# Seven-block products in single-bank PSUM tiles with four groups in flight

## The chip, the cores and the metric

The kernel runs on one core of a Trainium2 chip. The time is what the device takes for one execution, in microseconds (us); the median of several runs is given. The core's engines work side by side, each through its own list of instructions in order, and wait for each other by semaphores: TensorE (PE in the profile, with the weight loads as PEld), VectorE (DVE), ScalarE (ACT), GpSimd (POOL) and SyncE (SP). PE writes its results to PSUM, a memory of eight banks; here one bank holds 512 float32 numbers in each of 128 partitions. DVE and ACT read PSUM and write to the on-chip memory SBUF.

## The reference

```python
batch, n_heads, seq, head_dim = (8, 12, 448, 64)      # d_model = 768, d_ff = 3072

scores = scale * np.matmul(q, k.transpose(0, 1, 3, 2))
attn = np.maximum(scores, 0.0) ** 2 / S
attn_out = np.matmul(attn, v)

x = attn_out.transpose(0, 2, 1, 3).reshape(B, S, H * D)
xn = (x - mu) / np.sqrt(var + 1e-06) * g_ln
ch = np.maximum(xn @ w_ch1, 0.0) @ w_ch2
out = x + ch
```

`mu` and `var` are the mean and the variance over the 768 features of a row. Inputs and output are float32; the kernel multiplies in bfloat16 and sums in float32.

## The kernel before

Eight batches are worked through one after the other. For each there are the attention, the centring of its output, the first feed-forward product (the rows times w_ch1, then relu, into the activations `h1`) and the second (`h1` times w_ch2, scaled by the row's 1/sqrt(var) and added to x). The division by the standard deviation is pulled out of the first product and done at the end. Attention of a later batch is laid between the feed-forward steps of an earlier one. The last batch has no such filler left: its first product stands alone, and the last pass of second products follows it.

**Who sets the order.** The whole program is recorded by a planner, `Order`. Work for PE is added one step at a time by `pe`; work for the other engines is put in a list by `add`, with a cost, its dependencies and a key, and the planner commits it when its planned clocks say that it is next. The result is one fixed list for each engine. The planner's costs and due times decide only this order; on the chip, an instruction waits for the semaphores of what it reads and writes, and for all that stands ahead of it on its engine.

**The stage of the change.** For the last batch the first product is done by a scheme with seven block products in place of eight. The 24 column blocks of w_ch1 make six groups (`G4 = 6`). A group covers 4 x 128 columns of the output and all 448 rows of x; its output is cut in 2 x 2 blocks C11, C12, C21, C22 (two column halves, two halves of 224 rows). The products are P1, P2, P6, P5, P7, P3 and P4, each of 2 x 3 matmuls of 128x128 weights with 224 columns. Their operands are blocks or sums of blocks, made ahead on DVE: S1 to S4 of the weights (`make_w1_sums`), T1 to T4 of the rows (`make_x_sums`). In a group they run in four stages (`STAGES`): P1 P2, then P6 P5, then P7 P3, then P4. Two PSUM accumulators are used, x (P1, then P6, P7 and P4 added on) and y (P2; then P5 anew; then P3 added on). Between the stages:

- `keep` copies on ACT (L1128): c1 is x after P1, c2 is x after P6, p5 is y after P5; c1 and p5 go to a tile `v_t`, c2 to `at_all`, three places each.
- `add_relu` adds on DVE (L1112), with the relu in the same instruction: C11 = relu(y + c1) after P2, C22 = relu(x + p5) after P7, C12 = relu(y + c2) after P3.
- `relu` on ACT (L1141): C21 = relu(x) after P4.

P6 needs c1 (its accumulator may only be written on once the copy is taken), P5 needs C11, P7 needs c2, P3 needs p5, and P4 needs C22. Both accumulators of a group lie in one tile of two banks, from a pool `ps_s` of three such tiles that attention uses too. Two more banks, the pool `ps_f` (`f_tile`, `f_banks`), serve the other feed-forward products. The order of the stages over the groups is made beforehand by `fs_steps`, which plays the groups through with three places (`free`), 575 ns for a product and a given time until a group may go on.

**The last pass.** After the six groups, `ffn_w` does the second product for two pairs of row tiles with seven block products each (`PRODUCTS`), 12 matmuls of 384 columns to a product, in two halves (L1331; at the very end L1397). Its operands S1 to S4 are differences of activations, made on DVE (L1287); its results are taken out of PSUM by DVE (L1339), with the reciprocal root `r_t` (L805 on ACT, L807 on DVE, from the statistics L795 to L797) and stored by DMAs that ACT and SP issue (L1460). The statistics read rows of x that SP transposes by DMA (L772). For the pass before, the lines are L1422 and L1438.

`hold(slot_use)` marks a PSUM tile as taken until the group's last readers are known. `ops["h", b, i]` says to the planner when block i of the activations is ready.

Of the kernel before, what the change touches and what calls it, by code (L numbers as in the profile page):

```python
# [202 lines left out]
def kernel(  # L203
# [11 lines left out]
    P = 128  # L215
    bf16 = mybir.dt.bfloat16
    fp32 = mybir.dt.float32
# [3 lines left out]
    B, H, S, D = q.shape  # L221
# [26 lines left out]
    v_pool = ctx.enter_context(tc.tile_pool(name="v", bufs=1))  # L248
    xc_pool = ctx.enter_context(tc.tile_pool(name="xc", bufs=1))
    s_pool = ctx.enter_context(tc.tile_pool(name="small", bufs=4))  # L250
    ps_s = ctx.enter_context(tc.tile_pool(name="ps_s", bufs=3, space=bass.MemoryType.PSUM))
    ps_f = ctx.enter_context(tc.tile_pool(name="ps_f", bufs=1, space=bass.MemoryType.PSUM))

    identity = const_pool.tile([P, P], bf16)
    eps_sb = const_pool.tile([P, 1], fp32)
# [6 lines left out]
    sum_t = const_pool.tile([P, S], fp32)  # L262
# [29 lines left out]
    stage, vt, qkT, xc, xm, mvs, rstd = {}, {}, {}, {}, {}, {}, {}  # L292
    ops = {}
# [152 lines left out]
    slots = [DONE] * 3  # L446

    f_banks = [DONE] * 2
    f_tags = ["f0", "f1"]

    def f_tile(shape, dtype, **kw):

        f_tags.append(f_tags.pop(0))
        f_ps = ps_f.tile(shape, dtype, tag=f_tags[-1], **kw)
        return f_ps
# [11 lines left out]
    def hold(use):  # L467

        h = [PENDING]
        use(h)  # L470
        return h
# [3 lines left out]
    def later(*key):  # L475

        return later_ops.setdefault(key, [PENDING])

    def now_known(op, *key):
        later(*key)[:] = [op]  # L480
# [405 lines left out]
    def h_cols(b):  # L886
        return slice(T, T + S) if b % 2 == 0 else slice(0, S)
# [74 lines left out]
    G4 = K2 // 4  # L962
    SH = S // 2
    KQ = K1 // 2
    w1q = {}
    w1_todo = []
    f1q = {}

    def w1_block(g, row, k_half):
        return w1[:, k_half * KQ:(k_half + 1) * KQ, (4 * g + 2 * row) * P:(4 * g + 2 * row + 2) * P]  # L970
# [75 lines left out]
    W_OF = {"P1": ("A", 0, 0), "P2": ("A", 0, 1), "P6": "S2", "P5": "S1", "P7": "S3", "P3": "S4", "P4": ("A", 1, 1)}  # L1046
    X_OF = {"P1": "B11", "P2": "B21", "P6": "T2", "P5": "T1", "P7": "T3", "P3": "B22", "P4": "T4"}

    def fs_steps(b):

        order, live, t, nxt, free = [], {}, 0.0, 0, [0.0] * 3
        while nxt < G4 or live:
            ready = sorted(g for g, (st, r) in live.items() if r <= t)
            if ready:
                g = ready[0]
            elif nxt < G4 and min(free) <= t:
                g = nxt
                free.remove(min(free))
                live[g] = (0, t)
                nxt += 1  # L1060
            else:
                t = min([r for _, r in live.values()] + ([min(free)] if nxt < G4 and free else []))
                continue
            st = live.pop(g)[0]
            order.append(("fs", b, g, st))
            t += 575.0 * len(STAGES[st])
            if st < 3:
                live[g] = (st + 1, t + 1100.0)
            else:
                free.append(t + 1000.0)  # L1070
        return order

    def fs_deps(b, g, st, p=0):
        e = f1q.get(g, {})
        name = STAGES[st][p]
        w = W_OF[name]
        d = [ops["w1q", g, w] if isinstance(w, str) else None, ops["xq", X_OF[name]] if X_OF[name] in ("T1", "T2", "T3", "T4") else None]
        if st == 0:
            return [x for x in d if x is not None] + [ops["xc", b]] + ([slots[0]] if p == 0 else [])
        before = {"P6": "c1", "P5": "C11", "P7": "c2", "P3": "p5", "P4": "C22"}[name]  # L1080
        return [x for x in d if x is not None] + [e[before]]

    def ffn_1_seven(b, g, st):

        e = f1q.setdefault(g, {})
        for p, name in enumerate(STAGES[st]):
            bank = "x" if name in ("P1", "P6", "P7", "P4") else "y"

            def emit(eng, name=name, bank=bank):
                if name == "P1":  # L1090
                    ps = ps_s.tile([P, 2, 512], fp32, tag="s")
                    for i, x in enumerate("xy"):
                        e["ps", x] = ps[:, i, :S].rearrange("p (a c) -> p a c", a=2)
                w, x = W_OF[name], xq[X_OF[name]]
                a = w1q[g, w] if isinstance(w, str) else w1_block(g, *w[1:])
                for n in range(2):
                    for k in range(KQ):
                        nc.tensor.matmul(e["ps", bank][:, n, :], a[:, k, n * P:(n + 1) * P], x[:, k, :],  # L1098
                                         start=name in ("P1", "P2", "P5") and n == 0 and k == 0, stop=k == KQ - 1,
                                         skip_group_check=True)  # L1100
            op = R.pe(575.0, emit, fs_deps(b, g, st, p))
            e[name] = op
            if name == "P1":
                e["slot"] = hold(slot_use)
        c0 = h_cols(b).start

        def h_out(row, half):
            return h1[:, 4 * g + 2 * row:4 * g + 2 * row + 2, c0 + half * SH:c0 + (half + 1) * SH]

        def add_relu(key, row, half, bank, i1, deps):  # L1110
            def emit(eng):
                nc.vector._custom_dve(TENSOR_ADD_SAT, out=h_out(row, half), in0=e["ps", bank], in1=kept(i1), s0=float("inf"), s1=0.0)  # L1112
            e[key] = R.add("DVE", 620.0, emit, deps + [e[i1]], key=-3.0)

        def kept(name):
            if name == "c2":
                o = 3 * 2 * P + 3 * KQ * SH + (g % 3) * 2 * S
                t = at_all[:, o:o + 2 * S].bitcast(fp32)
            else:
                if "v" not in f1q:  # L1120
                    v_t = v_pool.tile([P, 3, S], fp32, tag="v1")
                    f1q["v"] = v_t
                t = f1q["v"][:, g % 3]
            return t.rearrange("p (a c) -> p a c", a=2)

        def keep(name, bank, deps):
            def emit(eng):
                nc.scalar.copy(kept(name), e["ps", bank])  # L1128
            e[name] = R.add("ACT", 560.0, emit, deps + [later("av_done", b)], key=-3.0)
        if st == 0:  # L1130
            keep("c1", "x", [e["P1"]])
            add_relu("C11", 0, 0, "y", "c1", [e["P2"]])
        elif st == 1:
            keep("c2", "x", [e["P6"]])
            keep("p5", "y", [e["P5"]])
        elif st == 2:
            add_relu("C22", 1, 1, "x", "p5", [e["P7"]])
            add_relu("C12", 0, 1, "y", "c2", [e["P3"]])
        else:
            def relu(eng):  # L1140
                nc.scalar.activation(h_out(1, 0), e["ps", "x"], Act.Relu)  # L1141
            e["C21"] = R.add("ACT", 560.0, relu, [e["P4"]], key=-3.0)
            e["slot"][:] = [e["C12"], e["C21"]]
            for i in range(4):
                ev = [e["C11"], e["C12"]] if i < 2 else [e["C21"], e["C22"]]
                ops["h", b, 4 * g + i] = ev
                later("h", b, 4 * g + i)[:] = ev
            if g == G4 - 1:
                ops["f1_end", b] = op
# [359 lines left out]
    def av_of(n):  # L1509
        return [("AV", n, s) for s in range(J)]  # L1510
# [118 lines left out]
    with tc.manual_schedule():  # L1629
# [32 lines left out]
        for c in FIRST_ORDER:  # L1662
            p = (av_stream if c == "a" else qk_stream).pop(0)
# [24 lines left out]
        for b in range(2, B):  # L1688
            u = b // 2
            vis = []  # L1690
            if b + 1 < B:
                n0 = (b + 1) * NPER
                for n in range(n0, n0 + NPER):
                    w = period(n, n > n0 or b > 2, False)
                    vis += w[1:] if n == n0 and b > 2 else w
                vis += [period(n0 + NPER, True, False)[0]] if b + 2 < B else [av_of(n0 + NPER - 1)]
            hooks = [(0, lambda b=b: load_batch(b + 2))] if b + 2 < B else []
            if b == 2:
                now_known(later("f2_out", 0), "s2_free", 1, 0)
            f2 = fw_steps(u, [0]) + f2_steps(u, [2]) if b % 2 == 0 else fw_steps(u, [3, 5])  # L1700
            for m in [0] if b % 2 == 0 else [3, 5]:
                pair_start(u, m)
            f1 = f1_steps(b)
            if b == LAST_B - 1:
                hooks = [(2, make_w1_sums)] + [(i, next_w1_sum) for i in range(4, 4 + 2 * 10, 2)] + [
                    (K2 + i, next_w1_sum) for i in range(14)]
            elif b == LAST_B:
                while w1_todo:
                    next_w1_sum()
                make_x_sums(b)  # L1710
                f1 = fs_steps(b)
            segment(f1 + f2, vis, b + 1 if b + 1 < B else None, 9000.0, hooks=hooks)
        R.drain()

# [29 lines left out]
```

## Time and profile before

| | us |
|---|---|
| three runs | 523.95, 523.54, 523.76 |
| median | 523.76 |
| the profiled execution, its own time | 524.23 |
| span in it, from the first to the last instruction | 522.5 |
| the last batch's seven-block products, first matmul to the last pass | 464.55 to 491.29 |
| the last pass on PE, with its closing products | 491.29 to 518.8 |

The other groups of this stage, by line, engine, operation and shape (tile names, shapes and count; busy us and mean ns of one; idle time of the engine before them and who ended it):

```profile
L1112 DVE CUSTOM_DVE_ANT_0 h<-ps,v_t 128x448 bf16<-128x448 f32 x12 | 7.4, 620 | 8.4 <-PE ps L1098 6.0 <-ACT v_t L1128 2.3
L1128 ACT COPY v_t<-ps 128x448 f32<-128x448 f32 x12 | 6.4, 535 | 8.1 <-PE ps L1098 8.1
L1128 ACT COPY at_all<-ps 128x448 f32<-128x448 f32 x6 | 3.2, 532 | 3.4 <-PE ps L1098 3.4
L1141 ACT ACTIVATE h<-ps 128x448 bf16<-128x448 f32 x5 | 2.7, 543 | 7.0 <-PE ps L1098 6.9
```

A row such as the first says: twelve adds on DVE, 620 ns each, 7.4 us in all; ahead of them DVE stood idle for 8.4 us, of which 6.0 were ended by PE's products and 2.3 by ACT's copies. The length of a matmul in the profile is modelled and reaches over the start of the next one, so how far apart two matmuls are is read from their starts.

### The profile page before, as it was taken

What the parts mean: (1) busy time and instruction counts of PE and PEld (TensorE: products, weight loads), DVE (VectorE), ACT (ScalarE), POOL (GpSimd) and SP (SyncE); (2) the same over time, 40 slices, a digit from 0 to 9 for tenths busy, and PEclk for the clock granted to TensorE, in tenths of its full rate; (3) what the DMA queues carried; (4) which work ended last, traced back from release to release, by engine and by line L of the source; (5) the groups of instructions that cost most, each with busy time, mean ns of one, the idle gap of its engine ahead of it and who ended that gap; (6) DMA issues with size and microseconds to landing.
All of it is one profiled execution on the core that took longest, in us unless ns stands there. A gap on an engine that the chain in (4) does not pass through costs nothing.

```text
span 522.5 us, 10193 instructions
## 1 busy us (share of the span) xinstructions
PE 507.8 (97%) x4200; PEld 285.9 (55%) x4200; DVE 371.1 (71%) x693; ACT 226.8 (43%) x365; POOL 116.4 (22%) x130
## 2 busy tenths in 40 slices
PE   5899999999999999999999999999999999999997
PEld 3444455555555455554555555554556555578764
DVE  5988647738897768774878667848488677968653
ACT  5977622116314663265522564336541476123300
POOL 6420700301141312321250311503211012300000
PEclk9999999999999999999999999999999999999999
DMA  9999999997279901989059960989224400231022
GB/s 193 197 186 195 202 195 155 172 126 105 63 113 184 100 7 19 166 128 107 15 102 113 128 78 15 148 122 95 38 39 93 92 0 1 54 83 19 1 60 62
DMA packets 144602, 51.85 MB, mean 99 GB/s; under 512 B 121894, under 2 KB 142764, under 8 KB 144556
## 3 DMA queue, kind: packets, MB, share of 16 engines
q0 software_dynamic: 81072, 25.50, 45.6%
q1 hardware_dynamic: 58844, 18.82, 21.7%
q10 hardware_dynamic: 4640, 6.88, 4.5%
q8 instruction: 33, 0.54, 0.4%
q14 instruction: 13, 0.11, 0.1%
HBM read 51.91 MB, written 11.01 MB: 120 GB/s over the span
## 4 chain that ended last, share of the span: by engine, by line
PE 89%; DVE 7%; ACT 2%; DMA 1%; issue 1%; SPq 0%; DVEq 0%; ACTq 0%
PE f_ps L934 37%; PE f_ps L1331 25%; PE f_ps L1422 10%; PE sc L590 6%; PE ps L653 5%; PE ps L1098 3%; DVE at_all L614 2%; DMA f<-in_k_dram 1%; DVE h L1112 1%; ACT at_all L599 1%; DVE a L863 1%; PE ps L510 1%; DVE h L1287 1%; DVE t L369 0%; DVE x_all L1209 0%
## 5 line engine op out<-in xcount | busy, mean ns | idle before, releaser
L934 PE MATMUL f_ps<-a,w 128*128 128x448 bf16 x990 | 193.1, 353 | 0.0
L934 PEld LDWEIGHTS <-w 128*128 128x128 bf16 x990 | 94.2, 98 | 94.0 <-issue 9.0
L599 ACT ACTIVATE at_all<-sc 128x896 bf16<-128x896 f32 x115 | 100.6, 924 | 70.5 <-PE sc L590 70.3
L950 ACT ACTIVATE h<-f_ps 128x448 bf16<-128x448 f32 (+1 forms) x138 | 72.4, 525 | 87.0 <-PE f_ps L934 85.3
L614 DVE TENSOR_TENSOR at_all<-at_all 128x896 bf16<-128x896 bf16 x157 | 98.7, 665 | 3.1 <-ACT at_all L599 3.0
L1331 PEld LDWEIGHTS <-h 128*128 128x128 bf16 x708 | 68.5, 98 | 47.9 <-issue 3.2
L601 DVE TENSOR_SCALAR at_all<-sc 128x896 bf16<-128x896 f32 x44 | 47.9, 1088 | 41.0 <-PE ps L653 23.6
L1331 PE MATMUL f_ps<-w,h 128*128 128x384 bf16 x360 | 62.5, 326 | 0.0
L590 PE MATMUL sc<-t 64*64 64x448 bf16 x672 | 49.4, 367 | 2.9 <-DVE t L369 1.5
L744 POOL TENSOR_TENSOR sum_t<-sum_t,xT_all 128x384 f32<-128x384 f32 (+2 forms) x25 | 20.9, 834 | 87.8 <-ACT xT_all L367 87.8
L1422 PE MATMUL f_ps<-w,h 128*128 128x384 bf16 x240 | 40.3, 326 | 0.0
L1339 DVE SCALAR_TENSOR_TENSOR o_all<-f_ps,r_t,x_all 128x384 f32<-128x384 f32 x39 | 24.0, 615 | 14.8 <-PE f_ps L1331 14.5
L590 PEld LDWEIGHTS <-t 64*64 64x64 bf16 x672 | 18.7, 107 | 27.8 <-issue 19.6
L1422 PEld LDWEIGHTS <-h 128*128 128x128 bf16 x240 | 23.2, 98 | 16.1 <-issue 1.1
L367 ACT CAST xT_all<-ps 128x768 bf16<-128x768 f32 (+2 forms) x32 | 19.9, 630 | 25.8 <-PE ps L653 23.7
L653 PE MATMUL ps<-at_all,v_t 64*64 64x448 bf16 x552 | 29.8, 350 | 0.0
L407 POOL DMA_DIRECT2D t<-in_k_dram x12 | 20.0, 1899 | 42.3 <-DMA t<-t 42.0
L742 POOL TENSOR_TENSOR sum_t<-xT_all 128x384 f32<-128x384 bf16 (+2 forms) x13 | 10.9, 860 | 81.8 <-ACT xT_all L367 81.5
L1339 DVE SCALAR_TENSOR_TENSOR o_all<-f_ps,r_t,o_all 128x384 f32<-128x384 f32 x30 | 18.4, 614 | 13.5 <-PE f_ps L1331 13.3
L653 PEld LDWEIGHTS <-v_t 64*64 64x64 bf16 x672 | 19.7, 107 | 13.5 <-issue 2.8
L407 POOL DMA_DIRECT2D t<-in_q_dram x12 | 19.3, 1772 | 32.9 <-DMA t<-t 29.8
L389 POOL DMA_DIRECT2D v_t<-in_v_dram x16 | 10.7, 674 | 63.1 <-PE sc L590 46.0
(135 smaller groups left out, 530.7 us busy)
## 6 DMA issues: line engine op xcount, KB each, us to landing
v_t<-in_v_dram POOLq DMA_DIRECT2D x16, 336.0 KB, 6.4
w<-in_moe_w_ch_dram POOLq DMA_DIRECT2D x4, 1152.0 KB, 37.9
out_dram<-o_all ACTq DMA_DIRECT2D x43, 96.0 KB, 2.8
t<-in_q_dram POOLq DMA_DIRECT2D x12, 336.0 KB, 7.8
t<-in_k_dram POOLq DMA_DIRECT2D x12, 336.0 KB, 6.8
out_dram<-o_all SPq DMA_DIRECT2D x35, 96.0 KB, 2.3
w<-in_moe_w_ch_dram POOLq DMA_DIRECT2D x4, 768.0 KB, 19.6
out_dram<-o_all ACTq DMA_DIRECT2D x13, 192.0 KB, 2.7
```

The lines of the kernel that those rows point to most:

```text
L407: nc.gpsimd.dma_start(stage["cols"][half * T:(half + 1) * T, t if b < 4 else 0].rearrange("p j (h d) -> p j h d", d=D), src[b, half * 6:ha ...
L590: nc.tensor.matmul(sc[rows_of(half), r, :S], qkT[b][rows_of(r), 1, s * NPER + pn, rows_of(half)], qT[:, :, pn, rows_of(half)], start=True, ...
L599: nc.scalar.activation(attn[n, s], st[0][:, :, :S], Act.Relu, scale=rc2)
L601: nc.vector.tensor_scalar(attn[n, s], st[0][:, :, :S], rc2, 0.0, op0=Alu.mult, op1=Alu.max)
L614: nc.vector.tensor_mul(attn[n, s], attn[n, s], attn[n, s])
L653: nc.tensor.matmul(av_st[n][half][rows_of(hh)], vt[b][rows_of(half), 2 * pn + hh, s * D:(s + 1) * D], attn[n, s][rows_of(half), hh, :], st ...
L744: nc.gpsimd.tensor_add(s0, s0, x0)
L934: nc.tensor.matmul(st[0], w1[:, ki, ni * P:(ni + 1) * P], xc[b][:, ki, :], start=(i == 0), stop=(i == K1 - 1))
L950: nc.scalar.activation(o, st[0][:, c], Act.Relu)
L1331: nc.tensor.matmul(e["ps", bank], a(k), w(k), start=new and k == 0, stop=k == KH - 1, skip_group_check=True)
L1339: nc.vector.scalar_tensor_tensor(o, e["ps", bank], r, o if more else xm[u, m + tile_n][:, cols], op0=Alu.mult, op1=Alu.add)
L1422: nc.tensor.matmul(o_st["ps"], stat(u, m, ki), w2[:, ki, j * hd:(j + 1) * hd], start=(ki == 0), stop=(ki == K2 - 1))
```

## The change

Five things are done. (1) A group's accumulators x and y become two tiles of one bank each, from a new pool `ps_n` that is opened in the place of `ps_s` when that is closed, at the first group; a tile of it waits only for what used its own memory. (2) Four groups may be under way in place of three (`FLIGHT`); the fourth of them, group 3, takes the two `ps_f` banks and a fourth place for the kept copies (`sum_t`, and a fourth part of `at_all`). (3) `fs_steps` counts on 1700 ns in place of 1100 and 1000 until a group may go on or its place is free (`AWAY`). (4) A block of activations counts as ready only with all blocks ahead of it. (5) The first half product of the last pass is laid ahead of the last block of the seven-block stage. The pool `ps_f` is now opened before `ps_s`, so the two change banks.

```diff
-    ps_s = ctx.enter_context(tc.tile_pool(name="ps_s", bufs=3, space=bass.MemoryType.PSUM))
     ps_f = ctx.enter_context(tc.tile_pool(name="ps_f", bufs=1, space=bass.MemoryType.PSUM))
+    s_banks = ctx.enter_context(ExitStack())
+    ps_s = s_banks.enter_context(tc.tile_pool(name="ps_s", bufs=3, space=bass.MemoryType.PSUM))
...
+    FLIGHT = 4
+    AWAY = 1700.0
+
     def fs_steps(b):
-        order, live, t, nxt, free = [], {}, 0.0, 0, [0.0] * 3
+        order, live, t, nxt, free = [], {}, 0.0, 0, [0.0] * FLIGHT
...
-            elif nxt < G4 and min(free) <= t:
+            elif nxt < G4 and free and min(free) <= t:
...
             if st < 3:
-                live[g] = (st + 1, t + 1100.0)
+                live[g] = (st + 1, t + AWAY)
             else:
-                free.append(t + 1000.0)
+                free.append(t + AWAY)
         return order
+
+    def in_f_banks(g):
+        return g == FLIGHT - 1
...
         if st == 0:
-            return [x for x in d if x is not None] + [ops["xc", b]] + ([slots[0]] if p == 0 else [])
+            return [x for x in d if x is not None] + [ops["xc", b]] + ([] if p else list(f_banks) if in_f_banks(g) else [slots[0]])
...
                 if name == "P1":
-                    ps = ps_s.tile([P, 2, 512], fp32, tag="s")
-                    for i, x in enumerate("xy"):
-                        e["ps", x] = ps[:, i, :S].rearrange("p (a c) -> p a c", a=2)
+                    if in_f_banks(g):
+                        x_ps = f_tile([P, S], fp32)
+                        y_ps = f_tile([P, S], fp32)
+                    else:
+                        if "pool" not in f1q:
+                            s_banks.close()
+                            f1q["pool"] = s_banks.enter_context(tc.tile_pool(
+                                name="ps_n", bufs=1, space=bass.MemoryType.PSUM, reuse_waits="tile"))
+                        x_ps = f1q["pool"].tile([P, S], fp32, tag=f"x{g % FLIGHT}")
+                        y_ps = f1q["pool"].tile([P, S], fp32, tag=f"y{g % FLIGHT}")
+                    for x, o in (("x", x_ps), ("y", y_ps)):
+                        e["ps", x] = o.rearrange("p (a c) -> p a c", a=2)
...
             if name == "P1":
-                e["slot"] = hold(slot_use)
+                e["x free"], e["y free"] = [hold(f_use) for _ in range(2)] if in_f_banks(g) else [hold(slot_use)] * 2
...
             if name == "c2":
-                o = 3 * 2 * P + 3 * KQ * SH + (g % 3) * 2 * S
+                o = 3 * 2 * P + 3 * KQ * SH + (g % FLIGHT) * 2 * S
                 t = at_all[:, o:o + 2 * S].bitcast(fp32)
             else:
...
-                t = f1q["v"][:, g % 3]
+                t = sum_t if g % FLIGHT == 3 else f1q["v"][:, g % FLIGHT]
...
-            e["slot"][:] = [e["C12"], e["C21"]]
+            e["x free"][:] = [e["C12"], e["C21"]]
+            e["y free"][:] = [e["C12"], e["C21"]]
+            f1q["out"] = ev = f1q.get("out", []) + [e[c] for c in ("C11", "C12", "C21", "C22")]
             for i in range(4):
-                ev = [e["C11"], e["C12"]] if i < 2 else [e["C21"], e["C22"]]
                 ops["h", b, 4 * g + i] = ev
...
                 f1 = fs_steps(b)
+                f1[-1:-1] = [f2.pop(0)]
             segment(f1 + f2, vis, b + 1 if b + 1 < B else None, 9000.0, hooks=hooks)
```

## The prediction

> **What bounds the kernel now.** I read the page first, then the busy table of the changed stage, then the order of its instructions in time, then the chain of waits.
>
> ```profile
> PE 507.8 (97%) x4200; PEld 285.9 (55%) x4200; DVE 371.1 (71%) x693; ACT 226.8 (43%) x365; POOL 116.4 (22%) x130
> PEclk9999999999999999999999999999999999999999
> PE 89%; DVE 7%; ACT 2%; DMA 1%; issue 1%; SPq 0%; DVEq 0%; ACTq 0%
> ```
>
> TensorE (PE) is busy for 97% of the span at full granted clock, so only time in which PE stands still can be won. The change touches one stage, the seven-block products of the last batch (L1098). It begins at 464.55 us and the last pass (L1331) follows it at 491.29. Busy time of PE, PEld (the weight loads), DVE, ACT and POOL in that stretch, then clock and DMA:
>
> ```profile
> 464.55:491.29 26.74, 25.42 (x254) 24.13 (x253) 17.63 (x36) 11.85 (x24) 0.00 (x0) 1.00 0.20 38
> ```
>
> There are 42 blocks (six groups of seven products) of six matmuls each. How long a block takes, and where PE stands, is read from starts, in the list of instructions by time:
>
> ```profile
> 467.71 0.74 PE L1098 MATMUL ps<-a,t 128*128 128x224 bf16 x6
> 468.29 0.74 PE L1098 MATMUL ps<-at_all,big_t 128*128 128x224 bf16 x6
> 468.86 0.74 PE L1098 MATMUL ps<-a,big_t 128*128 128x224 bf16 x6
> ...
> 471.23 0.74 PE L1098 MATMUL ps<-a,big_t 128*128 128x224 bf16 x6
> ...
> 472.16 0.73 PE L1098 MATMUL ps<-at_all,w 128*128 128x224 bf16 x6 [0.20 <-DVE h L1112]
> ```
>
> A block that follows without a stop starts 0.575 us after the one before (0.58, 0.57). 471.23 to 472.16 is 0.93, a stop of 0.36, of which the row admits 0.20: the drawn length of a matmul holds its way through the array. Over the whole stage: 42 x 0.575 = 24.15, and 26.74 - 24.15 = **2.59 us of stops**. Start by start they are 0.29 (at 467.14), 0.07, 0.36, 0.64 (at 476.25), 0.07, 0.36, 0.35, 0.07, 0.30 and 0.11, in sum 2.62. From 491.29 on, 156 matmuls of 384 columns take 25.35 us to 516.64, 0.1625 each, with no stop. So 2.59 is all that the change can win.
>
> Who is waited for is in the chain of waits (start, length, what):
>
> ```profile
> 464.71 1.16 PE ps L1098 x12
> 465.87 0.02 issue
> 465.90 0.54 ACT v_t L1128
> 466.44 0.02 issue
> 466.46 0.64 DVE h L1112
> 467.10 0.04 issue
> 467.14 3.69 PE ps L1098 x36
> ```
>
> The copy c1 reads P1's result but starts only after P2 (12 matmuls), since both lie in one tile; C11 follows on DVE; P6, which needs c1 alone, waits for C11 too.
>
> **The change part by part.**
>
> *Prices of a hand-over, from these rows.* P2's last matmul starts at 465.60 and the copy at 465.90, so from the end of a block's issue (last start + 0.10) to its reader are 0.20 us. The copy takes 0.535, DVE's add 0.62, and PE starts 0.05 to 0.06 later. So a block may start 0.78 us after its producer through ACT, 0.88 through DVE, if the reader's engine is free.
>
> *Single-bank tiles.* x and y no longer wait for each other: c1 starts a block earlier, P6 waits for c1 alone, P4 for C22 and no longer for C12 (0.55 behind it on DVE: 470.95, 471.50).
>
> *Four in flight.* The built order, blocks counted from 0: P1 P2 of groups 0, 1, 2 (0 to 5), P6 P5 of 0, 1, 2 (6 to 11), P7 P3 of 0, 1, 2 (12 to 17), P4 of 0 and 1 (18, 19), P1 P2 of 3 (20, 21), P4 of 2 (22), P1 P2 of 4 (23, 24), P6 P5 of 3 (25, 26), P1 P2 of 5 (27, 28), P6 P5 of 4 (29, 30), P7 P3 of 3 (31, 32), P6 P5 of 5 (33, 34), P7 P3 of 4 (35, 36), P4 of 3 (37), P7 P3 of 5 (38, 39), P4 of 4 (40), half of the last pass's first product, P4 of 5 (41), the other half. In blocks 0 to 40 each waits for one at least five before it, so four blocks, 2.30 us, lie between, against 0.78 or 0.88: at least 1.42 spare with a free reader. Laid end to end (block n at 464.55 + 0.575 n) and with DVE's and ACT's instructions put in their built order at their durations, the spare time is 2.0 to 2.1 in the first twelve dependent blocks and never under 1.4 up to block 40, though two pairs of S3 differences (1.03 a pair) and four statistics (1.2 each) stand between DVE's adds. All ten stops go: **-2.59 us**.
>
> *The end of the stage.* The half product (six matmuls, 0.975) writes a bank of group 3, so it waits for ACT's C21 of group 3, which is ready 0.78 after block 37; blocks 38 to 40 last 1.73: 0.95 spare. Block 41 waits for group 5's C22 on DVE, which has the fourth statistics and C12 of group 4 ahead of it. I place C12 at 487.12 and C22 at 487.66, done 488.28, and block 41 would start at 488.99: **0.65 spare, the least of the stage**. Behind it on PE stand the other half and all the last pass; without this cover each 0.1 us that DVE is later costs 0.1. P6 of the last pass follows at 492.49. It needs S2, whose second half now ends at 490.88 (after the last C21), and c1, done at 491.45: 0.98 spare. The square root and reciprocal move from 486.3 to 488.9, 1.9 before their first use. The stores and transposes keep their places in ACT's and SP's queues, and POOL issues nothing here.
>
> *Costed at nothing, with the cover.* The new pool's tiles wait for old readers: the last, the copy of the mean into sum_t, ends at 455.6, nine us early. Group 3 waits for both f banks: their eviction ends at 465.4, block 20 starts at 476.05. sum_t as fourth kept buffer: its readers, the subtractions, end at 459.6, the first write comes at 476.7. The fourth c2 slot lies where attention has finished. If a cover went, the price would be the lateness itself. The readiness list and the two constants reach the chip only through the order above. Before 464.55 the two programs agree instruction by instruction; only which bank is whose differs. Over the stage PE changes from 224 to 384 columns and back once more than before; the change shown costs nothing (the seven-block row that ends at 491.29 is followed at once), and the smallest stop in the list, 0.07, bounds it above: 0 to 0.14, taken as 0.
>
> *More signals on PE.* With one tile per block PE raises a semaphore after each of 42 blocks, before after 24. Blocks behind a raise start 0.572 to 0.578 after the last, others 0.575, so 18 more cost -0.05 to +0.05; I take 0. The Trainium skill speaks against: "TensorE: Matmul & The Clock Gate", section "The cost: per-tile semaphore tail", says that raises serialize at 26.3 ns each. By it 18 raises would cost 0.47 us and the time would be 521.64; the rows show no such cost behind matmuls of this length, and the sum goes by the rows.
>
> A second rule of the Trainium skill bears on how much there is to win. "Perfetto Trace Analysis", section "Identifying the Most-Contended Engine", holds that matmul busy time judges PE badly and weight-load busy time well. Here the former leaves 26.74 - 25.42 = 1.32 us (time 522.44), the latter 26.74 - 24.13 = 2.61 (521.15); the starts side with the latter.
>
> *Sum.* 523.76 - 2.59 = **521.17 us**. The durations come from a profiled execution of 524.23 (span 522.45, 1.78 outside it), 0.47 above the median of 523.76; in its terms the span falls to 519.86. Block pace (0.572 to 0.578, +-0.13 over 42), raises (+-0.05), column changes (+0.14) and the scatter of the runs (523.54 to 523.95, -0.22 to +0.19) give 520.8 to 521.7 for this case.
>
> **The rivals.**
>
> *One class of stop stays.* The copies and C11 give 0.29 + 0.64 + 0.35 = 1.28 of the 2.62; the largest, at 476.25, came from DVE being behind with S3 and statistics, which the change moves but doesn't remove. If these three stay, 523.76 - 2.62 + 1.28 = 522.42. For: DVE's work in the stage is still some 17.6 us in 24.2. Against: the adds concerned now have over 1.4 spare.
>
> *Given back in the last pass: no change.* P6 there waits for S2 and c1 on DVE. If DVE leaves the stage 0.98 + 2.59 = 3.57 us later than laid out, the win is lost: 523.76. For: S2's second half hangs on the very last C21. Against: DVE idles about 1 us ahead of it, so no backlog reaches it.
>
> *Slower: statistics hold DVE in front of the adds.* The second statistics wait for a transpose of x that SP issues at 465.95 and that lands 8.0 us later, at 474.0; I place them at 480.6, with C11 of group 5 and the rest behind them on DVE's one queue and PE's blocks behind those. Up to 6.6 us later landing costs nothing, the next 1.4 are spare, and from 480.6 + 1.4 + 2.59 = 484.6 on the kernel is slower than before; landing at 486 gives 521.17 + 4.0 = 525.2. For: a new order on DVE. Against: SP's queue is the same, and before, DVE waited for no DMA in this stage.
>
> **How the numbers follow.** All stops go 0.83; one class stays 0.08; no change 0.05; slower 0.04. About 0.2% (1.05 us) can be told from no change, so the first two (under 522.71) are faster: 0.91, 0.05, 0.04. The range takes the likeliest case and reaches towards the second: 520.7 to 522.2.
>
> **What would show it.** Right: the seven-block matmuls without a stop, 24.1 + 0.98 us from the first to the last with a half product between, weight loads busy throughout, each c1 copy starting 0.2 after P1 instead of P2, nothing lost after. Wrong: starts more than 0.6 apart, above all ahead of block 41, the half product or P6 of the last pass, with DVE as releaser; a block pace above 0.578; or DVE idle until a DMA.

## The result, and the profile after

| | before | after |
|---|---|---|
| runs taken with the first result, median | 523.86 us (523.54 to 524.34, 4 runs) | 520.76 us (520.25 to 521.04, 4 runs) |
| ratio of them, 95% interval | | 0.9939 (0.9922 to 0.9956) |
| a repeat with more runs, median | 523.71 us (11 runs) | 521.09 us (520.61 to 521.94, 5 runs) |
| ratio of the repeat, 95% interval | | 0.9948 (0.9935 to 0.9960) |
| profiled execution, span | 522.5 us | 519.1 us |
| in it: first seven-block matmul | 464.55 us | 463.85 us |
| in it: from there to the start of the last matmul | 54.01 us | 51.42 us |

The kernel is faster, and by more than was forecast in the first comparison: 3.1 us where 2.59 stood in the prediction. The last two rows split what the profile shows. The changed stage and all behind it became 54.01 - 51.42 = 2.59 us shorter, the sum of the prediction. Another 0.70 us lie ahead of the stage, where the two programs issue the same instructions. The two spans differ by 3.33 us in all (the 3.38 in one of the expectations below is a slip).

The page of after, busy time and the engines' shares of the chain that ended last:

```profile
PE 506.2 (98%) x4200; PEld 286.1 (55%) x4200; DVE 370.4 (71%) x693; ACT 227.5 (44%) x365; POOL 116.4 (22%) x130
...
PE 91%; DVE 5%; ACT 1%; DMA 1%; issue 1%; ACTq 0%; DVEq 0%
```

The stage of after, from its first matmul to the end of its last block, with half a product of the last pass in it (length; PE, PEld, DVE, ACT, POOL busy; clock; DMA):

```profile
463.85:488.98 25.13, 25.13 (x261) 24.74 (x259) 17.89 (x37) 12.59 (x24) 0.00 (x0) 1.00 0.24 41
```

42 x 0.575 + 0.975 = 25.13 us: PE is busy for the whole stretch. Before, PE was drawn busy for 25.42 of 26.74 us while its starts showed 2.59 us of stops; now both say none.

The first instructions of the stage after, by time (start, length, engine, line, tiles, count, idle time and who ended it):

```profile
463.85 0.74 PE L1114 MATMUL x_ps<-a,w 128*128 128x224 bf16 x6
...
464.43 0.74 PE L1114 MATMUL y_ps<-a,w 128*128 128x224 bf16 x6
464.63 0.53 ACT L1144 COPY v_t<-x_ps 128x448 f32<-128x448 f32 x1 [4.42 <-PE x_ps L1114]
...
465.32 0.62 DVE L1128 CUSTOM_DVE_ANT_0 h<-y_ps,v_t 128x448 bf16<-128x448 f32 x1 [0.64 <-PE y_ps L1114]
```

The copy c1 starts 0.20 us after P2 begins, that is, after P1 has been issued; before, it came after P2, 1.35 us behind the stage's start in place of 0.78. C11 then waits for y, not for the copy, and starts 0.32 us after P2 has been issued (465.00 to 465.32).

The end of the chain of waits of after (start, length, what):

```profile
487.01 0.58 PE x_ps L1114 x6
487.59 0.97 PE f_ps L1348 x6
488.57 0.57 PE x_ps L1114 x6
489.14 24.37 PE f_ps L1348 x150
513.51 1.99 PE f_ps L1414 x24
```

Between the stage's start and the closing DVE add no other engine is left in it. The DVE and ACT pieces that stood between PE's before are gone.

### The profile page after: what moved, and what is told of

Its sections match the earlier page's. It is cut to its first block, busy times and chain, and to the rows that moved or that the text cites. A ratio compares the mean times of both kernels' runs of the same rounds, so it can differ in the third digit from the quotient of the medians.

```text
span 519.1 us, 10197 instructions
## 1 busy us (share of the span) xinstructions
PE 506.2 (98%) x4200; PEld 286.1 (55%) x4200; DVE 370.4 (71%) x693; ACT 227.5 (44%) x365; POOL 116.4 (22%) x130
## 4 chain that ended last, share of the span: by engine, by line
PE 91%; DVE 5%; ACT 1%; DMA 1%; issue 1%; ACTq 0%; DVEq 0%
PE f_ps L935 37%; PE f_ps L1348 25%; PE f_ps L1439 10%; PE sc L591 7%; PE ps L654 5%; PE x_ps L1114 2%; PE y_ps L1114 2%; DVE at_all L615 1%; PE f_ps L1114 1%; DVE t L370 1%; ACT at_all L600 1%; DMA f<-in_q_dram 1%; PE ps L511 1%; DVE x_all L1226 0%; PE f_ps L915 0%
```

## The experiments

Where the extra half microsecond came from, and which part of the change took the 2.59, were the open questions. All but the last two kernels were timed against the kernel before, in two sets, each with runs of before of its own. The exchanged banks, the single-bank tiles alone, the new order with shared tiles and the kernel without the half product go by 523.95 us (522.83 to 525.46, 21 runs). The others go by 523.71 us (523.18 to 524.78, 11 runs). "Stretch" is the time from the first seven-block matmul to the start of the last matmul in the kernel's profile; it doesn't see what happens ahead of the stage.

**Banks exchanged, nothing else.**

```diff
-    ps_s = ctx.enter_context(tc.tile_pool(name="ps_s", bufs=3, space=bass.MemoryType.PSUM))
     ps_f = ctx.enter_context(tc.tile_pool(name="ps_f", bufs=1, space=bass.MemoryType.PSUM))
+    ps_s = ctx.enter_context(tc.tile_pool(name="ps_s", bufs=3, space=bass.MemoryType.PSUM))
```

> The kernel before with only the two PSUM pools opened in the other order, so that each has the banks that the other had. The profiled executions of before and after differ by 3.38 us in span, of which 2.59 arise in the seven-block stage and 0.70 ahead of it (0.40 by the first transposes, 0.57 by 32 us), where the two programs differ in nothing but the banks. Theory S (scatter of the first loads): the time is that of before within 0.2%, ratio 0.999 to 1.001, the stage has its 2.6 us of stops, and its first matmul falls anywhere between 463.7 and 464.7. Theory B (the exchange of banks quickens the earlier stages): ratio 0.9985 or less, about 0.5 us, and the stage starts near 463.9 with its 2.6 us of stops.

Measured: 523.86 us, ratio 0.9998 (0.9987 to 1.001); stage start 464.25, stretch 54.01, the ten stops as before. Theory B falls.

**The changed kernel once more.**

> The changed kernel once more, unaltered, with more rounds. Theory S (the half microsecond beyond 2.59 was scatter of the part ahead of the stage): the gain over before goes down towards 2.6 us, ratio near 0.995, median near 521.3; in the profile the stretch from the first seven-block matmul to the last matmul is 51.4 us again (before 54.0), wherever the stage starts between 463.4 and 464.8. A rival (the change truly gives 3.1 us): the ratio stays at 0.994 or below and the median near 520.8.

Measured: 521.09 us, ratio 0.9948 (0.9935 to 0.9960), 2.62 us between the medians; stage start 464.06, stretch 51.42. The gain went down towards the 2.59, as theory S has it. The first interval (0.9922 to 0.9956) holds 0.9951, which is 2.59 of 523.9, and the second doesn't exclude 0.994, so the timed runs alone would not settle it; the profiles do. In the ten of this study (before, after and the eight experiments) the stage starts between 463.37 and 464.82; the one with the old banks, at 464.55, lies among the others. From a product near 164 us on, the stage is reached in 300.11 to 300.13 us in all ten. Nearly the whole scatter arises earlier, in three places: the second half of the transposes at 8 us (0.36 to 1.92 us between two matmuls, which wait for the first k rows), a scores product at 127 us (0.26 to 0.77) and a product of an earlier batch at 152 us (0.16 or 0.72). A fourth, at 31.8 us, moved in one of the ten alone (0.47, else 0.19). Without these four waits the stage's starts would lie within 0.13 us of each other, in place of 1.45.

The timed runs can be asked the same: take from each median the stretch of that kernel's profile, and what is left is the rest of the kernel, ahead of the stage and after the last matmul's start. Against its own runs of before, this rest is 0.51 us less in the first comparison (469.85 to 469.34) and 0.03 less in the repeat. In the exchanged banks, and in the four kernels below that were timed, it goes from 0.30 less to 0.45 more. A gain that the change made outside the stage should show in the repeat and in all four; there is none in common, and the 0.51 is little more than what comes and goes without a cause in the stage.

Two chains of waits show the first, with the kernel before and then with the single-bank tiles of the next experiment:

```profile
1.77 5.67 DMA f<-in_k_dram
...
7.46 0.44 DVE t L369
...
7.95 0.52 PE f_ps L510 x11
```

```profile
1.76 6.83 DMA f<-in_k_dram
...
8.62 0.44 DVE t L370
...
9.10 0.52 PE f_ps L511 x11
```

The same load, issued at the same time, takes 1.16 us longer to land, and the transposes start 1.15 later. In the profile of after it lands 4.5 us after its issue and isn't in the chain at all.

**Single-bank tiles alone.**

```diff
-    FLIGHT = 4
+    FLIGHT = 3
...
-                live[g] = (st + 1, t + AWAY)
+                live[g] = (st + 1, t + 1100.0)
...
-                free.append(t + AWAY)
+                free.append(t + 1000.0)
...
-        return g == FLIGHT - 1
+        return False
...
-            f1q["out"] = ev = f1q.get("out", []) + [e[c] for c in ("C11", "C12", "C21", "C22")]
...
+                ev = [e["C11"], e["C12"]] if i < 2 else [e["C21"], e["C22"]]
...
-                f1[-1:-1] = [f2.pop(0)]
```

> Single-bank tiles alone: three groups, the old due times, the old readiness, no half product ahead. Theory T (the shared tile made the stops): laid out as in the prediction, one stop of some 0.24 us is left, at the last block of a group, behind DVE; the stage takes 24.4 us instead of 26.7 and the kernel 2.3 to 2.4 us less than before. Theory F (the fourth group made the room): more than 1 us of stops stays and the kernel gains under 1.6 us.

Measured: 521.49 us, ratio 0.9953 (0.9936 to 0.9969); stretch 51.53, so 2.48 of the 2.59 us. One stop is left, of 0.11 us in place of the 0.24 expected. It is behind DVE, as expected, but ahead of a P5 and not of the last block of a group. Its place in the timeline:

```profile
473.07 1.03 DVE L1304 TENSOR_TENSOR h<-h 128x768 bf16<-128x768 bf16 x2 [0.47 <-ACT h L1157]
...
474.01 0.56 DVE L796 BATCH_NORM_STATS2 st<-x_all 128x6 f32<-128x384 bf16 x1
...
474.59 0.74 PE L1114 MATMUL y_ps<-a,w 128*128 128x224 bf16 x6
...
475.17 0.74 PE L1114 MATMUL x_ps<-at_all,big_t 128*128 128x224 bf16 x6
475.19 1.14 DVE L1128 CUSTOM_DVE_ANT_0 h<-y_ps,v_t 128x448 bf16<-128x448 f32 x2
475.85 0.54 PE L1114 MATMUL y_ps<-a,big_t 128*128 128x224 bf16 x4
```

475.17 to 475.85 is 0.68, a stop of 0.11: P5 waits for C11, and C11 stands on DVE behind the differences and the statistics. Before, it was the block just ahead of this one, P6 of the same group, that stood for 0.64 us, waiting for C11 only because of the shared tile. Nine of the ten stops go with the single-bank tiles alone, and 0.11 us is left of the tenth; theory F falls.

**Three groups, all else as changed.**

```diff
-    FLIGHT = 4
+    FLIGHT = 3
...
-        return g == FLIGHT - 1
+        return False
```

> The changed kernel with three groups in flight in place of four, all else kept (single-bank tiles, the due time of 1700, readiness, the half product ahead of the last P4). Laid out as in the prediction there is no stop: 51.4 us from the first seven-block matmul to the last matmul, the same time as the changed kernel. Theory F (the fourth group is needed): stops of 0.3 us or more, 0.3 us or more above the changed kernel.

Measured: stretch 51.42, no stop; 521.57 us, ratio 0.9957 (0.9943 to 0.9971), and its profile's stage start is 464.10. The fourth group isn't needed. Its median lies 0.48 above the changed kernel's, the intervals overlap, and the part that the two differ in takes the same 51.42 us.

**The new order with shared tiles.**

```diff
-                        if "pool" not in f1q:
-                            s_banks.close()
-                            f1q["pool"] = s_banks.enter_context(tc.tile_pool(
-                                name="ps_n", bufs=1, space=bass.MemoryType.PSUM, reuse_waits="tile"))
-                        x_ps = f1q["pool"].tile([P, S], fp32, tag=f"x{g % FLIGHT}")
-                        y_ps = f1q["pool"].tile([P, S], fp32, tag=f"y{g % FLIGHT}")
+                        both = ps_s.tile([P, 2, 512], fp32, tag="s")
+                        x_ps, y_ps = both[:, 0, :S], both[:, 1, :S]
```

> The changed kernel's order, four groups, half product and readiness, but x and y of a group in one tile of two banks again (group 3 keeps its two tiles). Theory F: no stop, the same time as the changed kernel. Theory T with distance: the new order keeps four blocks between a product and the next on its tile, which hides most of the longer wait; one stop of 0.9 us is left, ahead of the last P4, which now waits for C12 as well; 1.6 to 1.7 us less than before. Theory T alone, without help from the order: 2 us or more of stops.

Measured: 521.97 us, ratio 0.9967 (0.9955 to 0.9979); stretch 52.33, 1.68 less than before, with one stop of 0.91 us:

```profile
486.66 0.57 DVE L1124 CUSTOM_DVE_ANT_0 h<-both,at_all 128x448 bf16<-128x448 f32 x1
...
487.28 0.73 PE L1110 MATMUL both<-at_all,w 128*128 128x224 bf16 x6 [0.75 <-DVE h L1124]
487.28 0.48 PEld L1110 LDWEIGHTS <-w 128*128 128x128 bf16 x5 [0.91 <-issue]
```

That is P4 of group 4, released by C12, which doesn't touch its accumulator. The size is the expected one; the place is not, for the stop was expected ahead of the last P4, that of group 5. Distance in the order hides the shared tile's longer waits everywhere but there. Tiles and order are two cures for the same stops: alone they give 2.48 and 1.68, together 2.59. The 1.68 is the order with the half product in it and with group 3 in two tiles of its own. The weight loads' idle time (0.91) shows the whole stop, PE's drawn idle time 0.75 of it.

**Without the half product ahead of the last P4.**

```diff
-                f1[-1:-1] = [f2.pop(0)]
```

> The changed kernel without the half product of the last pass ahead of the last P4. The prediction put 0.65 us of spare time there with 0.975 us of cover; without the cover a stop of 0.33 us ahead of the last P4, with DVE as releaser, and 0.3 us more than the changed kernel. A rival that the cover is not needed: no stop.

Measured: stretch 51.72, 0.29 more than the changed kernel; 521.70 us, ratio 0.9956 (0.9941 to 0.9971). The stop is where it was expected, ahead of the last P4. DVE's C22 ends at 488.48, and the weight loads go on at 488.54:

```profile
487.87 0.61 DVE L1128 CUSTOM_DVE_ANT_0 h<-x_ps,v_t 128x448 bf16<-128x448 f32 x1
...
488.54 0.48 PEld L1114 LDWEIGHTS <-w 128*128 128x128 bf16 x5 [0.29 <-issue]
```

**DVE made late ahead of the last P4.** C22 of group 5 is computed once more, or three times more, over itself.

```diff
-                nc.vector._custom_dve(TENSOR_ADD_SAT, out=h_out(row, half), in0=e["ps", bank], in1=kept(i1), s0=float("inf"), s1=0.0)
+                for _ in range(2 if g == G4 - 1 and key == "C22" else 1):
+                    nc.vector._custom_dve(TENSOR_ADD_SAT, out=h_out(row, half), in0=e["ps", bank], in1=kept(i1), s0=float("inf"), s1=0.0)
```

> The changed kernel with C22 of group 5 computed twice on DVE, the second time over the first with the same numbers. 0.62 to 0.68 us more stand ahead of the release of the last P4, against 0.65 spare as laid out: a stop there of 0 to 0.1 us. If the spare time is a good deal larger, no stop; if there is none, 0.6 us.

> The same computed four times: some 2.0 us more on DVE ahead of the last P4, so a stop of 1.3 to 1.4 us there (2.0 less 0.65), DVE as releaser, and everything behind it on PE later by as much; the last pass gives none of it back. If the last pass could hide a late DVE, the last matmul would come less than 1.3 us later, counted from the first seven-block matmul.

Measured: with one more, no stop and a stretch of 51.42 (one run, 521.0 us); the second C22 ends at 488.40 and P4 starts at 488.48, so next to nothing is spare. With three more, a stop of 1.29 us, a stretch of 52.72, 1.29 longer (one run, 522.23 us). The place in the changed kernel, then with three more:

```profile
487.05 0.61 DVE L1128 CUSTOM_DVE_ANT_0 h<-x_ps,v_t 128x448 bf16<-128x448 f32 x1
...
488.40 0.74 PE L1114 MATMUL x_ps<-at_all,w 128*128 128x224 bf16 x6
```

```profile
487.08 2.59 DVE L1129 CUSTOM_DVE_ANT_0 h<-x_ps,v_t 128x448 bf16<-128x448 f32 x4
...
489.73 0.74 PE L1114 MATMUL x_ps<-at_all,w 128*128 128x224 bf16 x6 [1.13 <-DVE h L1129]
```

C22 ends at 487.66 and PE could follow at 487.72: 0.68 us spare before 488.40. Three more adds make DVE 1.98 later, and 1.98 - 0.68 = 1.30. The last pass gives none of it back.

## Why the prediction was right or wrong

- **The size of the stops, 2.59 us**: right. The stretch became 2.59 us shorter.
- **"All ten stops go"**: right; blocks 0 to 40 start 0.575 us apart throughout, with 42 raises in the stage, so the raises cost nothing that can be seen, as the rows had it. The 0.47 us by "TensorE: Matmul & The Clock Gate" of the Trainium skill, section "The cost: per-tile semaphore tail", did not come; that section fits its figure to small tiles packed side by side, and these blocks are 128x128 matmuls of 224 columns.
- **The spare time ahead of the last P4, 0.65**: measured 0.68, by the profile and by the two late kernels. The cover of half a product is worth 0.29 us (0.33 by the same sum; 0.975 - 0.68 gives the 0.29). The agreement of 0.65 and 0.68 is partly luck: counted from the stage's start, C22 was placed to end at 23.73 us and the last P4 to start at 24.44, and they came at 23.81 and 24.55. The prediction's own pace, 41 x 0.575 + 0.975, gives the 24.55.
- **"At least 1.42 spare"** in blocks 0 to 40: mis-sized, without effect. The 0.20 us from a block's issue to its reader was read from a copy on ACT and used for DVE too, but DVE's adds start 0.30 to 0.32 us after the issue (465.00 to 465.32; 484.55 to 484.86). For P4 of group 4, C22 ends at 485.48 and the block starts at 486.85; with the 0.06 for the hand-over to PE, 1.31 us were spare, the least of these blocks.
- **The parts**: the prediction named single-bank tiles and four groups side by side and gave their sum only. The tiles alone bring 2.48; the fourth group adds nothing that the profile shows.
- **One class of stop stays; no change; slower by statistics**: none came. DVE waited for no transpose in the stage.
- **The step that failed** is a term of the range: "the scatter of the runs (523.54 to 523.95, -0.22 to +0.19)". Three runs were too few for it: over the 36 timed runs of before in this study the time goes from 522.83 to 525.46, the stage's start moves by 1.45 us between profiles, and the interval of the first comparison is 0.9 us wide to either side. The first comparison, 3.1 us, exceeds 2.59 by more than that term allows: by its ratio the time is 0.9939 x 523.76 = 520.57, under the low end of 520.7. (The median as it stands, 520.76, lies 0.06 inside it, and the repeat, 521.09, is 0.08 from the forecast.) That the excess is scatter, and not a gain, rests on the constant stretches (2.59 us less in each of the four profiles without stops, 300.1 us from 164 us to the stage in all ten), on the repeat (2.62 us), on the exchanged banks (ratio 0.9998) and on the rest of the kernel, which moves by up to 0.45 us in the other timed kernels without a gain common to them. What makes the load at 1.8 us land early or late, no run here shows. The prediction counted "which bank is whose" as free, and it is, within 0.13%. The profile of before held a warning that was not used: a load of 5.67 us stands in its chain of waits at 1.8 us, and what hangs on a load may move from run to run.

## What to carry to other kernels

A wait is as wide as the tile that the dependency is kept on: two accumulators that lay in two banks all along, but in one tile, made PE wait for readers of the other one. Split the tile before adding buffers, and read PE's loss from the starts of its matmuls or from the weight loads' idle time, not from PE's drawn idle time. When a gain of half a per cent is forecast, compare the stretch that was changed as well as the whole time, and take the scatter from more than three runs.

## What was not expected of the hardware

Two DVE adds of 128x384 bfloat16 elements near 150 us take either 0.35 us each or 1.57 and 1.06, and that decides the stop at 152 us. Here are the kernel before, with POOL's adds beside them and PE's stop behind them, and the single-bank tiles alone, without the stop:

```profile
149.28 2.56 DVE L1209 TENSOR_TENSOR x_all<-w,a_t 128x384 bf16<-128x384 bf16 x2
...
149.69 0.94 POOL L744 TENSOR_TENSOR sum_t<-sum_t,xT_all 128x384 f32<-128x384 f32 x1
150.71 0.92 POOL L745 TENSOR_TENSOR rsum_t<-sum_t,xT_all 128x384 bf16<-128x384 f32 x1
...
152.42 1.30 PE L1331 MATMUL f_ps<-t,h 128*128 128x384 bf16 x7 [0.40 <-DVE o_all L1339]
```

```profile
150.12 0.62 DVE L1226 TENSOR_TENSOR x_all<-w,a_t 128x384 bf16<-128x384 bf16 x2
...
150.52 0.99 POOL L745 TENSOR_TENSOR sum_t<-sum_t,xT_all 128x384 f32<-128x384 f32 x1
151.59 1.22 POOL L746 TENSOR_TENSOR rsum_t<-sum_t,xT_all 128x384 bf16<-128x384 f32 x1
```

PE waits for a DVE instruction that stands behind the two adds (`o_all`). Both engines have the same lists here in all ten profiles, and DVE's first add starts 0.40 to 0.41 us ahead of POOL's in every one, so the phase between them doesn't tell the two forms apart. What does is not shown. The slow form stood in six of the ten profiles (before, the exchanged banks, the changed kernel twice and both late ones), the quick one in the other four. The Trainium skill, "SBUF — State Buffer", section "SBUF: two separate sides", says that the two engines share a pair of ports which one of them holds for a whole instruction while the other stands. The slow rows fit that: each DVE add ends 0.2 us after one of POOL's (150.86 after 150.63, 151.84 after 151.63). In the quick form it is POOL's second add that is longer, 1.22 in place of 0.92. But by the same section whichever starts first gets the pair, and by the drawn starts that is DVE in both forms, so the rows don't show which engine held it. It was not tested by itself.
